# Turning the operands of a small DFT: the stationary side becomes x, column by column, and the table moves

## The chip, the cores and the metric

The kernel runs on one core of one Trainium2 chip. The metric is device time in microseconds (us), taken over several executions. The engines are named as in the profile: PE is TensorE (PEld its weight loads), DVE is VectorE, ACT is ScalarE, POOL is GpSimd, SP is SyncE. "Lxx" is a line of the kernel that was profiled. Line numbers differ from kernel to kernel, so the text says which line does what.

## The reference

```python
def _attn_ref(x):                       # x: 8 x 3136 x 256, float32
    X = np.fft.fft(x, axis=1)           # over the 3136 positions = 49 x 64
    X = np.fft.fft(X, axis=2)           # over the 256 features
    return X.real

def _moe_ref(x, U, V, w_ch1, w_ch2):    # U: 3136x32, V: 32x3136, w_ch1: 256x1024, w_ch2: 1024x256
    h = x.transpose(0, 2, 1) @ U @ V    # low-rank mixing over the positions
    u = x + h.transpose(0, 2, 1)
    return u + np.maximum(u @ w_ch1, 0) @ w_ch2
```

The transform over 3136 = 49 x 64 is done in two stages. The first is a DFT over the 49 rows n1 (position = 64 n1 + n2). It leaves, for each of the 64 values of n2 and each of 25 values of k1 (the rest follow by symmetry), one vector over the features d. The second stage is a DFT over n2. A matmul of this kernel sums over partitions (its stationary operand has 98 of them in the first stage, 2 x 49), so the first stage wants n1 on the partitions, and the second wants n2 there. What lies on the partitions for the second stage is called the *lines*: 32 cosine and 32 sine lines, because n2 and 64 - n2 are folded together.

## The kernel before

The batches are handled in four pairs. Pair 0 is special: its two batches go one after the other, so that PE has something to do early. For these the first stage is `s1_single`. The table is the stationary operand, x moves, and the result `z` has k1 and the cosine/sine index on the partitions and the lines along the free axis. To bring the lines onto the partitions, z is written to DRAM and read back (`turn`). The argument calls this round trip "the turn".

```python
    def load_single(b, c):                       # a quarter of one batch: 49 rows, and 49 mirrored rows
        ...
        nc.gpsimd.dma_start(out=xs[0:PR:2], in_=x_pn[r, 8 * c:8 * c + 8, :])
        mirror = bass.AP(x.tensor, x.offset + (b * S + N2 - 8 * c) * D, [[N2 * D, N1], [-D, 8], [1, D]])
        nc.gpsimd.dma_start(out=xs[1:PR:2], in_=mirror)
    ...
    def s1_single(pr, b, tiles, evacs, engines):
        def step(n, s):
            ...                                  # two column tiles of 64, in turn; 98x64 table stationary
                        nc.tensor.matmul(o, f, y, start=(m == 0), stop=True, skip_group_check=True)
            evacs[n](z[:, 2 * s:2 * s + 2, :], ps[:])
            if n % 2:
                ...                              # z to DRAM, two lines at a time
                    engines(n)[i].dma_start(out=dst, in_=z[64 * i:64 * i + 64, 4 * q:4 * q + 4]...)
        for n, s in enumerate([2, 3, 4, 5, 6, 7, 1, 0]):
            yield lambda n=n, s=s: step(n, s)

    def turn(pr, b, parts, engines=(nc.sync,)):
        g = gpool.tile([P, NK1, D], BF16, tag=f"g{b}", name="g")
        src = zd[pr.p % 2, b].rearrange("k cn d -> cn k d")
        for i, (k0, k1) in enumerate(parts):     # back from DRAM, lines on the partitions
            engines[i % len(engines)].dma_start(out=g[0:64, k0:k1], in_=src[:, k0:k1, :])

    def te_single(pr, b, spread):                # the product with U from g: tile "teps"
        ...                                      # then te is copied below g by "spread"
    def s3_steps(pr, b, evac):                   # second stage: g stationary, table T moving
        ...
```

After that come the two MLP products (`hps`, `ops`), in chunks. Each pair has 52 slots, and `plan` hangs other work on the slots. For pair 0 it places the work of the second batch (batch 1) thus:

```python
            place(s1_single(cur, 1, part[1], [copy_act, copy_dve] * 4, ...), 2, 10)
            place([lambda: turn(cur, 1, whole)], 10, 11)
            place([lambda: te_single(cur, 1, spread_pool)], 15, 16)
            place(s3_steps(cur, 1, copy_dve), 17, 29)
            place_next(pairs[1], 8, 2.6, 44)
```

The first batch (batch 0) is done before the slots begin, in what I call the front.

## Time and profile before

| | before |
|---|---|
| time, median of 3 executions (range) | 476.18 us (475.4 to 478.35) |
| span of the profiled execution | 472.8 us |
| PE busy | 440.1 us (93%) |
| first second-stage product (L290) | starts at 32.4 us |
| product with U of batch 1 (teps) ends | 81.7 us |

The first part of the page gives the busy time of each engine, its share of the span, and its instructions:

```profile
PE 440.1 (93%) x3831; PEld 310.1 (66%) x3831; DVE 224.4 (47%) x520; ACT 287.6 (61%) x387; POOL 139.0 (29%) x140
```

PE is nearly full on average. The places where it is not are the only ones that an early change can win. The chain of waits shows two of them. Its columns are the start, the duration, and what the time went to (lines that follow each other in the chain, cut to 0 to 85 us):

```profile
20.09 3.52 DMA zturn<-z
...
24.31 5.91 DMA g<-zturn
30.26 0.69 PE teps L266 x18
...
32.41 0.54 PE ps L290 x4
...
67.12 2.41 DMA zturn<-z
69.58 9.20 DMA g<-zturn
78.82 2.87 PE teps L266 x48
81.68 1.82 PE hps L341 x4
```

Twice the chain leaves PE and follows the turn: at 20 to 30 us for batch 0, and at 67 to 79 us for batch 1. The same shows in the waits of PE (line and what it waited for: us in total, times, longest), for 0 to 110 us:

```profile
PE teps L266 <- DMA g<-zturn: 6.8, 2, 6.5
```

The stop at 72 to 79 us costs more than its 6.5 us, because PE's granted clock is about half in the stretch behind it. A window shows it. Its columns are the stretch and its length, the busy time of PE, PEld, DVE, ACT and POOL (with instructions), then PE's granted clock (1.00 is full speed), the DMA share and GB/s:

```profile
79.00:84.00 5.00, 5.00 (x60) 3.61 (x57) 2.23 (x5) 0.46 (x1) 3.70 (x3) 0.53 0.71 201
```

At half clock the teps products take 2.87 us, and four hps matmuls take 1.82 us, not 0.97.

### The profile page before, as it was taken

What the parts mean: (1) busy time and instruction counts of PE and PEld (TensorE: products, weight loads), DVE (VectorE), ACT (ScalarE), POOL (GpSimd) and SP (SyncE); (2) the same over time, 40 slices, a digit from 0 to 9 for tenths busy, and PEclk for the clock granted to TensorE, in tenths of its full rate; (3) what the DMA queues carried; (4) which work ended last, traced back from release to release, by engine and by line L of the source; (5) the groups of instructions that cost most, each with busy time, mean ns of one, the idle gap of its engine ahead of it and who ended that gap; (6) DMA issues with size and microseconds to landing.
All of it is one profiled execution on the core that took longest, in us unless ns stands there. A gap on an engine that the chain in (4) does not pass through costs nothing.

```text
span 472.8 us, 9751 instructions
## 1 busy us (share of the span) xinstructions
PE 440.1 (93%) x3831; PEld 310.1 (66%) x3831; DVE 224.4 (47%) x520; ACT 287.6 (61%) x387; POOL 139.0 (29%) x140
## 2 busy tenths in 40 slices
PE   6679994899999999999999999999999999999993
PEld 2445663677767776677777767677767777767672
DVE  8965431767326366646244366654245345112111
ACT  6436561577755657677665656777565655666660
POOL 8442522945150054643060145452130000000000
PEclk9978997999999999999999999999999999999998
DMA  9969369678478366585493366584682222233323
GB/s 158 229 159 161 87 179 192 171 235 215 143 175 196 91 169 155 138 258 180 124 219 89 102 171 182 140 259 150 150 153 63 68 64 66 68 76 75 79 57 79
DMA packets 69298, 67.65 MB, mean 143 GB/s; under 512 B 17396, under 2 KB 62268, under 8 KB 69220
## 3 DMA queue, kind: packets, MB, share of 16 engines
q1 hardware_dynamic: 55252, 47.43, 40.9%
q0 software_dynamic: 11168, 12.92, 12.4%
q10 hardware_dynamic: 2832, 6.69, 3.9%
q8 instruction: 30, 0.49, 0.5%
q14 instruction: 16, 0.13, 0.1%
HBM read 35.95 MB, written 34.28 MB: 149 GB/s over the span
## 4 chain that ended last, share of the span: by engine, by line
PE 79%; DVE 8%; DMA 6%; ACT 3%; issue 2%; SPq 0%; DVEq 0%; ACTq 0%
PE hps L341 33%; PE ops L352 32%; DMA g<-zturn 5%; PE ops L355 4%; PE ps L290 4%; PE ps L172 2%; ACT hT L343 2%; DVE q L79 2%; PE teps L252 1%; DMA zturn<-z 1%; PE ps L216 1%; PE teps L266 1%; DVE ob L362 1%; ACT om L361 1%; DVE yb L122 1%
## 5 line engine op out<-in xcount | busy, mean ns | idle before, releaser
L343 ACT ACTIVATE hT<-hps 128x1024 bf16<-128x1024 f32 (+1 forms) x208 | 202.5, 975 | 138.3 <-PE hps L341 136.9
L352 PE MATMUL ops<-W,hT 128*128 128x256 bf16 x1568 | 224.6, 273 | 0.0
L352 PEld LDWEIGHTS <-hT 128*128 128x128 bf16 x1568 | 145.3, 98 | 34.4 <-issue 0.3
L362 DVE TENSOR_TENSOR ob<-ops,om 128x256 f32<-128x256 f32 (+1 forms) x100 | 41.8, 418 | 196.0 <-ACT om L361 194.2
L341 PE MATMUL hps<-q,W1p 128*128 128x512 bf16 (+1 forms) x448 | 106.7, 361 | 1.0 <-DVE q L79 0.7
L341 PE MATMUL hps<-q,W1m 128*128 128x512 bf16 x384 | 98.9, 381 | 0.5 <-ACT hT L343 0.5
L131 POOL TENSOR_TENSOR y<-xa,xb 98x1020 f32<-98x1020 f32 (+1 forms) x24 | 55.2, 2299 | 127.8 <-DMA xa<-in_x_dram 115.4
L79 DVE CAST q<-ps 128x512 bf16<-128x512 f32 (+3 forms) x120 | 64.4, 558 | 29.6 <-PE ps L290 26.6
L341 PEld LDWEIGHTS <-W1p 128*128 128x128 bf16 x448 | 40.4, 98 | 29.2 <-issue 4.7
L341 PEld LDWEIGHTS <-W1m 128*128 128x128 bf16 x384 | 35.8, 98 | 26.8 <-issue 2.2
L355 PEld LDWEIGHTS <-q 128*128 128x128 bf16 x392 | 38.5, 98 | 21.0 <-issue 0.3
L76 ACT CAST z<-ps 128x512 bf16<-128x512 f32 x57 | 33.4, 586 | 14.3 <-PE ps L172 12.5
L361 ACT COPY om<-ops 128x256 f32<-128x256 f32 (+1 forms) x100 | 36.8, 368 | 8.0 <-PE ops L352 7.6
L363 DVE TENSOR_TENSOR ob<-ops,om 128x256 f32<-128x256 f32 (+1 forms) x100 | 40.9, 409 | 0.0
L290 PE MATMUL ps<-T,g 128*128 128x128 bf16 (+1 forms) x400 | 38.2, 223 | 2.8 <-DVE g L274 1.5
L355 PE MATMUL ops<-Bp,q 128*128 128x128 f16 x200 | 38.4, 219 | 0.0
L355 PE MATMUL ops<-Bm,q 128*128 128x128 f16 x192 | 37.0, 219 | 0.0
L274 POOL COPY g<-te 64x1024 int32<-64x1024 int32 (+1 forms) x21 | 22.0, 1092 | 46.5 <-DVE te L238 46.5
L290 PEld LDWEIGHTS <-g 128*128 128x128 bf16 x400 | 30.3, 100 | 8.1 <-issue 2.0
L122 DVE TENSOR_TENSOR yb<-y 98x508 bf16<-98x508 f32 (+1 forms) x24 | 26.9, 1123 | 0.0
L102 POOL DMA_INDIRECT xb<-in_x_dram,idx x24 | 25.0, 1041 | 5.4 <-issue 3.9
L172 PE MATMUL ps<-yb,F 98*128 98x258 bf16 (+1 forms) x108 | 18.9, 265 | 4.9 <-DVE q L79 4.9
(126 smaller groups left out, 205.1 us busy)
## 6 DMA issues: line engine op xcount, KB each, us to landing
out_dram<-ob SPq DMA_DIRECT2D x392, 64.0 KB
xa<-in_x_dram SPq DMA_DIRECT2D x24, 392.0 KB
g<-zturn SPq DMA_DIRECT2D x7, 800.0 KB
zturn<-z ACTq DMA_DIRECT2D x9, 512.0 KB
xs<-in_x_dram POOLq DMA_DIRECT2D x16, 196.0 KB, 8.3
w_f<-in_moe_w_ch_dram SPq DMA_DIRECT2D x2, 1024.0 KB
zturn<-z SPq DMA_DIRECT2D x15, 128.0 KB
zturn<-z ACTq DMA_DIRECT2D x3, 448.0 KB
```

The source lines that it names most:

```text
L76: nc.scalar.copy(o, i)
L79: nc.vector.tensor_copy(o, i)
L122: nc.vector.tensor_tensor(o[:, :, 1:128], i[:, :, 1:128], i[:, :, 255:128:-1], op=AL.add)
L131: nc.gpsimd.tensor_tensor(ck.y[:, 0:n, 1:256], ck.xa[:, 0:n, 1:256], rb[:, :, 255:0:-1], op=AL.add)
L290: nc.tensor.matmul(o, lt, r, start=st, stop=True, skip_group_check=True)
L341: nc.tensor.matmul(ps[:, i, 0:n], (W1p if ch.sg > 0 else W1m)[:, blk, j], q[:, blk, c0:c0 + n], start=(blk == 0), stop=(blk == 1))
L343: nc.scalar.activation(ch.h[:, 2 * jp:2 * jp + 2, 0:n], ps[:, :, 0:n], AF.Relu)
L352: nc.tensor.matmul(ps, ch.h[:, j, t * P:(t + 1) * P], W2[:, j, :], start=(j == 0 and t % 2 == 0), stop=(j == JT - 1), skip_group_check=True)
L355: nc.tensor.matmul(ps[:, j], q[:, j, tk], (Bp if ch.sg > 0 else Bm)[:, j], start=False, stop=False, skip_group_check=True)
L361: nc.scalar.copy(om[:, 0:n], ch.po[:, 0:n, 1])
L362: nc.vector.tensor_tensor(ob[:, 0:n, 0:P], ch.po[:, 0:n, 0], om[:, 0:n], op=AL.add)
L363: nc.vector.tensor_tensor(ob[:, 0:n, P:D], ch.po[:, 0:n, 0], om[:, 0:n], op=AL.subtract)
```

## The change

The intent is to have the first stage's result come out of PE with the lines already on the partitions. For this x is the stationary operand: for each feature d, the 98 x 32 block X[0:98, :, d] is loaded as weights, and the table moves (50 columns, real and imaginary parts of 25 k1). The result's partitions are then the lines. Four 32-column tiles of the array are used in turn. A batch takes 512 pairs of a weight load and a matmul, in place of 8 steps with wide matmuls. The turn is gone for pair 0. What it needs in exchange: the whole of x of a batch in one tile before the first pair, line 32 on its own path, the lines in reversed order, and a row of signs in the table T. The diff, cut to its core:

```diff
-    def load_single(b, c):
...
+    def load_single(b):
+        X = zpool.tile([P, 32, D], BF16, tag="z", name="X")
+        nc.vector.memset(X[0:PR, 31, :].bitcast(FP32), 0.0)
...
+        rows(0, L, 33, 1, X[1:2 * L:2, 0:31, :])              # L = 48 rows
+        rows(0, L, 31, -1, X[0:2 * L:2, 0:16, :])             # 48 rows, lines backwards
+        rows(0, L, 15, -1, X[0:2 * L:2, 16:32, :])
+        rows(L, 1, 33, 1, X[PR - 1:PR, 0:31, :])              # the 49th row
+        rows(L - 1, 2, 31, -1, X[PR - 4:PR:2, 0:32, :])       # rows 48 and 49, backwards
+        nc.gpsimd.dma_start(out=x32[b][0:PR:2], in_=x_pn[r0:r0 + N1, 32, :])
...
-    def s1_single(pr, b, tiles, evacs, engines):
...
+    def turned_products(X, ps, i0, n):
+        for i in range(n):
...
+            for m in range(2):
+                for h in range(2):
+                    d = 64 * h + i0 + i
+                    for c in range(2):
+                        o = ps[64 * h + 32 * c:64 * h + 32 * c + 32, i]
+                        w = X[0:PR, :, (256 - d if d else 128) if m else d]
...
+                        nc.tensor.matmul(oc, w, f, start=first[2 * h + c], stop=True, skip_group_check=True)
...
+    def turned_out(g, ps, i0, n, evacs):
+        for h in range(2):
+            evacs[h](g[0:63]..., ps[64 * h:64 * h + 63]...)    # straight into g
...
+    trow = tmp([1, NK1, 64], "trow", BF16)                     # row of signs for T, by POOL
...
+    nc.sync.dma_start(out=T[63:64, :, 0:64], in_=trow[:])
...
+    sin_of(T[0:63, :, 0:64], ta2[0:63], 18)
...
     nc.vector.tensor_copy(T[0:64, :, 64:128], T[0:64, :, 63::-1])
+    for r in range(4):                                         # the front: batch 0, 128 pairs a round
+        ps = psh.tile([P, 16, 2, 32], FP32, tag="h", name="tps")
+        turned_products(X0, ps, 16 * r, 16)
+        turned_out(g0, ps, 16 * r, 16, [copy_dve, copy_act])
...
-    for c in (1, 2, 3, 0):
-        part[1][c] = load_single(1, c)
+    loads = load_single(1)                                     # at the end of the front
...
-            place(s1_single(cur, 1, part[1], ...), 2, 10)
-            place([lambda: turn(cur, 1, whole)], 10, 11)
+            place(turned_steps(cur, 1, X1, [copy_act, copy_dve]), 4, 12)   # batch 1, 64 pairs a step
```

The loads of w_ch1, w_ch2 and V also moved to POOL's queue, behind x.

## The prediction

> **What bounds the kernel now.** The page gives PE 93% of a 472.8 us span; from about 84 us on PE is hardly idle, and the change does not touch that part. What can be won lies in two waits for the first pair's turn through DRAM. (1) Front: the chain of waits shows zturn<-z 3.5 us, an issue of 0.6, then g<-zturn 5.9, until 30.2 us; the first mixing product that reads g (L290) starts at 32.4. (2) Batch 1: in the timeline PE stops at about 72 us and resumes with teps at 78.8, released by g<-zturn (6.6 us idle). The granted clock is then half: 50 teps matmuls take 2.87 us, the next four hps 1.89 instead of 1.03. I count 8.8 us in all. A like half clock covers 32.5 to 39.3 us (eight hps take 3.68 us).
>
> **Removed.** Both turns, eight evacuations a batch (0.59 to 0.69 us) and, for batch 1, eight first-stage steps of 0.56 us = 4.5 us of PE.
>
> **Added.** Per batch 512 small load-and-multiply pairs (98x32 stationary, 50 moving columns, four column tiles in turn), and evacuations of 400 or 800 elements: by the casts in the trace (512 elements 0.69 us on DVE, 0.59 on ACT) an estimated 0.6 and 1.1 us each, beside PE. The price of a pair decides. In the trace two column tiles start 2 to 4 ns apart and each streams at its own pace (254 columns every 108 ns); L252 sustains a pair per 27.9 ns, bounded by the array. [...] the uups matmuls here (64 columns, one tile) start 31.6 ns apart. [...] stationary columns 512 bytes apart and instruction fetch (256 instructions per 1.0 to 1.7 us packet here) should push it up. Estimate: 10 to 18 ns, centre 14, 7 us a batch.
>
> **On the critical path.** Front: products can start at about 17 us, when x has landed and the U products are through, and end near 24.5; then DVE still has the last evacuation, W1p (1.2 us), the residual tables (1.9), the T copies and teps before L290. I expect L290 at 31 to 32, hardly earlier. Batch 1: 8.8 + 4.5 - 7.2 = 6 us won. Against it: the turned products need all of X1, while before chunks were used as they landed. X1's loads (10 us of packets in front now) follow a DVE memset behind the te spreads, so X1 may land only at 45 to 49 us and PE may wait a few us at step 4. Net about 5 us.
>
> **Predicted: 471 us**, 8 in 10 between 461 and 481; faster by over 2% 0.32, within 2% 0.58, slower by over 2% 0.10.
>
> **What would show it.** zturn traffic of pair 0 gone; no PE gap before the second teps, full granted clock from 70 to 84 us; turned matmuls under 20 ns apart; L290 starting at 30 to 33 us with DVE as its releaser; a PE wait at the first batch-1 turned product, released by the X load; after 90 us the same lines as before.
>
> **What would make it wrong.** Pairs at 28 ns or more (14 us a batch: nothing left, or a loss); X1 so late that PE stalls over 5 us and loses the clock again; or pairs at 7 ns and a front 3 us shorter, which gives 462.

The marks stand where two passages on the price of a pair are cut: a figure that no run here shows, and a floor for a pair that was partly taken from it. The uups matmuls' 31.6 ns in one tile make 7.9 ns over four tiles, if four run side by side as two do at L252 (128 columns, at 254 columns in 108 ns, take 54 ns, so 27 ns a pair with two tiles; 27.9 were measured). What was added to that for the strides and the instructions, up to the centre of 14 ns, was the author's estimate. The sum itself came to 8.8 + 4.5 - 7.2 = 6 us won at batch 1 (7.2 us is 512 x 14 ns), about 5 us after a late X1: 476 - 5 = 471 us.

## The result, and the profile after

| | before (4 runs) | after (4 runs) |
|---|---|---|
| time, median (range) | 476.0 us (475.4 to 478.35) | 494.6 us (492.66 to 495.14) |
| ratio, with 95% interval | | 1.0371 (1.0327 to 1.0414), slower |
| span of the profiled execution | 472.8 us | 493.4 us |
| first second-stage product | 32.4 us (L290) | 45.0 us (L307) |
| product with U of batch 1 ends | 81.7 us | 102.5 us |

A ratio is the mean time of one kernel's runs over that of the other's runs of the same rounds, so not quite the ratio of the medians quoted. Executions over 1.5% slower than the fastest of the same kernel are left out of the means.

The last two rows of the table already locate the loss. It is 12.6 us at the first second-stage product and 20.8 us when the product with U of batch 1 ends. The spans differ by 20.6 us, so nothing is lost or won later. The page's first part shows 884 more matmuls on PE, each with its weight load:

```profile
PE 449.7 (91%) x4715; PEld 322.0 (65%) x4715; DVE 225.9 (46%) x524; ACT 290.4 (59%) x394; POOL 135.6 (27%) x134
```

The chain of waits after (the turn's lines are gone; other things stand in their place):

```profile
23.04 5.79 DMA T<-trow
28.92 0.58 DVE T L576
29.50 0.90 DVE g L80
...
31.30 4.82 PE tps L222 x223
36.15 0.99 DVE g L80
...
44.29 0.70 DVE g L291
45.04 0.57 PE ps L307 x4
...
50.98 0.53 POOL X L118
51.51 7.91 DMA X<-in_x_dram
59.42 2.57 issue
...
62.66 3.45 DMA x<-in_x_dram
...
101.01 1.52 PE teps L283 x47
```

And the waits of PE after:

```profile
PE ps L198 <- DMA x<-in_x_dram: 7.9, 1, 7.9
PE tps L222 <- ACT g L77: 5.8, 1, 5.8
PE ps L307 <- DVE g L291: 4.3, 1, 4.3
...
PE tps L222 <- issue: 2.4, 1, 2.4
```

Both early waits that the change was to remove are gone, and new ones have come. In the front, the rounds of pairs (tile tps, L222) run from 18.3 to 36.1 us, with a stop for the evacuations of two tiles (the copies from the accumulators into g). DVE copies one half of each tile and ACT, after it, the other; and in its order DVE stands before them at a copy of T (L576), which waits for the row of signs (28.83 us; the copy starts at 28.92, the first evacuation behind it at 29.50). From the last round to L307 pass another 9 us, about 7 on DVE and 2 on ACT. At batch 1, PE comes to the first product (L198, that of line 32) at 58.3 us and waits 7.9 us for the x of batch 1, called X1 here; its last load, the small one of line 32 (`x<-in_x_dram`), lands at 66.1 us. The window from 60 to 70 us shows the half clock again, now here:

```profile
60.00:70.00 10.00, 3.85 (x78) 2.61 (x78) 0.58 (x1) 1.23 (x3) 1.77 (x4) 0.52 0.21 25
```

In that window the DMA engines are nearly idle (25 GB/s), so X1 is late because it was asked for late. The timeline of POOL, which issues the loads, says why (start, us, engine, line, operation, count, and the idle time before with its releaser):

```profile
1.42 2.77 POOL L118 DMA_DIRECT2D X<-in_x_dram  x4
14.05 0.69 POOL L118 DMA_DIRECT2D X<-in_x_dram  x1 [9.86 <-DMA X<-in_x_dram]
...
50.98 2.53 POOL L118 DMA_DIRECT2D X<-in_x_dram  x4 [24.29 <-issue]
61.99 0.68 POOL L118 DMA_DIRECT2D X<-in_x_dram  x1 [8.49 <-issue]
```

Each batch has five loads into X, and line 32's behind them. The fifth, the small one with two rows, writes elements of partition 94 that the mirrored loads of 48 rows also write. I take this to be why POOL holds it, and everything that POOL has behind it, until those have landed (e5 below speaks for it: 2.97 us of waiting in place of 9.86). For batch 0 this delays all of POOL's later work by 9.9 us, the row of signs included; for batch 1 it comes on top of a late start, which a DVE memset at 50.3 us sets. There the view names no releaser for the 8.49 us, and the chain has the load before landed at 59.42 us, 2.57 us before POOL goes on; that rest is not explained.

### The profile page after: what moved, and what is told of

Read it like the earlier page. It is cut to its first block, busy times and chain, and to the rows that moved or that the text cites. A ratio compares the mean times of both kernels' runs of the same rounds, so it can differ in the third digit from the quotient of the medians.

```text
span 493.4 us, 11483 instructions
## 1 busy us (share of the span) xinstructions
PE 449.7 (91%) x4715; PEld 322.0 (65%) x4715; DVE 225.9 (46%) x524; ACT 290.4 (59%) x394; POOL 135.6 (27%) x134
## 2 busy tenths in 40 slices
DMA packets 59506, 64.02 MB, mean 130 GB/s; under 512 B 13764, under 2 KB 52510, under 8 KB 59326
## 3 DMA queue, kind: packets, MB, share of 16 engines
q1 hardware_dynamic: 49086, 41.61, 36.8%
q0 software_dynamic: 8208, 15.38, 13.4%
## 4 chain that ended last, share of the span: by engine, by line
PE 75%; DMA 6%; DVE 5%; ACT 3%; issue 3%; SPq 1%; POOL 0%; DVEq 0%; ACTq 0%
PE ops L369 30%; PE hps L358 30%; PE ops L372 4%; PE ps L307 4%; PE ps L222 2%; PE ps L179 2%; ACT hT L360 2%; DMA X<-in_x_dram 2%; DMA g<-zturn 1%; DMA out_dram<-ob 1%; PE teps L269 1%; DVE q L80 1%; DMA T<-trow 1%; PE tps L222 1%; SPq L384 1%
## 5 line engine op out<-in xcount | busy, mean ns | idle before, releaser
L372 PEld LDWEIGHTS <-q 128*128 128x128 bf16 x392 | 38.4, 98 | 22.1 <-issue 1.6
L307 PE MATMUL ps<-T,g 128*128 128x128 bf16 (+1 forms) x400 | 38.3, 223 | 6.6 <-DVE g L291 4.3
L372 PE MATMUL ops<-Bp,q 128*128 128x128 f16 x200 | 38.4, 219 | 0.0
L307 PEld LDWEIGHTS <-g 128*128 128x128 bf16 x400 | 30.4, 101 | 12.0 <-DVE g L291 4.5
L77 ACT CAST z<-ps 128x512 bf16<-128x512 f32 x48 | 28.2, 588 | 12.3 <-PE ps L179 12.1
L222 PEld LDWEIGHTS <-X 98*32 98x32 bf16 x1024 | 19.8, 172 | 10.3 <-issue 9.9
```

The lines of the kernel that those rows point to most:

```text
L77: nc.scalar.copy(o, i)
L222: nc.tensor.matmul(oc, w, f, start=first[2 * h + c], stop=True, skip_group_check=True)
L307: nc.tensor.matmul(o, lt, r, start=st, stop=True, skip_group_check=True)
L372: nc.tensor.matmul(ps[:, j], q[:, j, tk], (Bp if ch.sg > 0 else Bm)[:, j], start=False, stop=False, skip_group_check=True)
```

## The experiments

The causes that the result offered were put as theories. W: waits for late data (the row of signs behind POOL's wait, and X1) are the loss. D: the tail of DVE work between the last round and L307 is. F came up after the first experiments: PE isn't supplied with instructions fast enough. P: the pairs themselves cost more than the 14 ns predicted. The quoted expectations use these letters.

Twelve kernels ran, in four groups, each group on one chip with the kernel before beside it. The medians of before in the groups were 474.15, 473.23, 474.73 and 474.31 us. Ratios in this section are against those runs. The kernel "after" itself was not run again; where I subtract from its 494.6 us the numbers come from two chips, whose runs of before differ by 2 to 3 us.

| run | what | median us | ratio (95% interval) |
|---|---|---|---|
| e1_copy_late | after, T's copy behind the rounds | 494.44 | 1.0453 (1.0355 to 1.0550) |
| e2_no_overlap | after, mirrored loads of 47 rows | 613.18 | 1.2939 (1.2825 to 1.3053) |
| e3_load_early | after, X1 loaded right behind the rounds | 486.67 | 1.0274 (1.0163 to 1.0384) |
| e4_all_three | e1, e2 and e3 together | 600.04 | 1.2688 (1.2569 to 1.2807) |
| e5_tail_first | after, two-row load first | 488.88 | 1.0361 (1.0299 to 1.0424) |
| e6_three_mended | e1, e3 and e5 together | 481.60 | 1.0208 (1.0149 to 1.0268) |
| e7_twice | e6, batch 1's pairs done twice | 490.46 | 1.0386 (1.0307 to 1.0466) |
| e8_second_only | before, the change for batch 1 alone | 474.79 | 1.0075 (0.9998 to 1.0151) |
| e9_te_before_w1 | e6, front's tail reordered | 482.46 | 1.0163 (1.0111 to 1.0216) |
| e10_before_te_late | before, batch 1's U product four slots later | 485.07 | 1.0207 (1.0154 to 1.0259) |
| e11_contiguous | e6, stationary from neighbouring elements (wrong result) | 476.26 | 1.0029 (0.9980 to 1.0078) |
| e12_second_gathered | e8, DVE gathers the columns first | 487.60 | 1.0313 (1.0268 to 1.0358) |

### e1_copy_late: the copy that waits for the row of signs, moved away

```diff
-    nc.vector.tensor_copy(T[0:64, :, 64:128], T[0:64, :, 63::-1])
     g0 = gpool.tile([P, NK1, D], BF16, tag="g0", name="g")
...                                                            # the four rounds
+    nc.vector.tensor_copy(T[0:64, :, 64:128], T[0:64, :, 63::-1])
     nc.scalar.copy(T[64:96, 1:9, 64:128], Vk[64:96, 48:40:-1, :])
```

> One line moved: the mirrored copy T[0:64,64:128] on DVE goes behind the evacuations of the turned rounds, so that the late landing of the row of signs (T<-trow, 28.9 us) no longer holds the in-order DVE queue. Theory W (waits: the loss is three waits that the change brought in): the turned rounds no longer wait 5.8 us for an evacuation, L307 starts about 6 us earlier (39 instead of 45 us) and the time falls by 5 to 8 us, to 487-490. Theory P (price: the loss is the PE time of 1024 small pairs at 15 to 18 ns, 17 us, less the 9 us of steps they replaced): the rounds are as long as before in PE time, what is not waited for at the front is waited for later, and the time falls by less than 2 us.

It took 494.44 us: nothing won, although the wait for the evacuations (5.8 us) is gone. L307 starts at 45.3 us. The waits of PE name another thing in the same place, and the timeline of PE in e1 shows where it sits (start, us, engine, line, operation, tiles, shapes, count, and the idle time before with its releaser):

```profile
PE tps L222 <- issue: 6.7, 3, 3.1
```

```profile
24.58 2.53 PE L222 MATMUL tps<-Fs,X 98*32 98x50 f16 x128 [2.69 <-issue]
30.23 2.57 PE L222 MATMUL tps<-Fs,X 98*32 98x50 f16 x128 [3.12 <-issue]
33.68 2.40 PE L222 MATMUL tps<-Fs,X 98*32 98x50 f16 x121 [0.88 <-issue]
```

"issue" means that PE waited for nothing that the profile shows. The pauses come after every 128 pairs, which is 256 instructions. I worked out the next table from the trace: PE's start times, counted as instructions, and the packets of the queue that carries instructions (16,384 bytes each; the page of after lists 37 such packets, and 2 x 4715 / 256 = 36.8; for before it lists 30, and 2 x 3831 / 256 = 29.9; so a packet seems to hold 256 of PE's instructions).

```
e1: PE stops after instruction   from     to       for     packet on the instruction queue
             448                 21.67    24.58    2.91    21.79 to 23.04
             704                 26.86    30.23    3.37    27.83 to 28.95
             960                 32.55    33.68    1.13    31.33 to 32.39
```

The times are from the start of one instruction to the start of the next, so a little longer than the idle times above. Each stop has its packet: PE goes on 1.3 to 1.5 us after that packet has ended. This is theory F.

A round is 128 pairs too, so the stops might belong to the rounds. They do not: each comes 7 pairs into a round (512 - 121 - 128 - 128 = 135 = 128 + 7). The trace of after has both kinds of stop side by side, one at pair 135 without a releaser and one at pair 256, where a round ends, for the evacuation:

```profile
18.36 2.42 PE L222 MATMUL tps<-Fs,X 98*32 98x25 f16 x132
23.20 2.35 PE L222 MATMUL tps<-Fs,X 98*32 98x50 f16 x121 [2.42 <-issue]
31.30 4.79 PE L222 MATMUL tps<-Fs,X 98*32 98x50 f16 x256 [5.75 <-ACT g L77]
```

Behind the second the marks 704 and 960 pass without a stop: while PE stood still a packet had come (27.53 to 28.66 us), and the next (31.04 to 32.21) came in time. So the late row of signs had hidden the supply, since both hold PE at the same time. Of W, the part about the row of signs falls as a cause by itself.

### e2_no_overlap and e4_all_three: without the shared partition, by 47 rows

```diff
-        rows(0, L, 31, -1, X[0:2 * L:2, 0:16, :])
-        rows(0, L, 15, -1, X[0:2 * L:2, 16:32, :])
+        rows(0, L - 1, 31, -1, X[0:2 * L - 2:2, 0:16, :])
+        rows(0, L - 1, 15, -1, X[0:2 * L - 2:2, 16:32, :])
```

> The two big mirrored loads of X take 47 rows instead of 48, so that the two-row load behind them writes no partition that they write. Theory W: POOL no longer waits 9.9 us at its fifth load; kio, V, the weights and the row of signs are all issued about 8 us earlier, T<-trow lands before 22 us; L307 starts 5 to 8 us earlier. For batch 1 the load of x32 is issued at about 54 instead of 62.7 us and the first turned product starts some 3 us sooner after the loads begin. Time down by 7 to 11 us, to 484-488. Theory P: down by less than 2 us.

> All three edits. Theory W, with the pairs still at their price: L307 starts at 36 to 39 us (before the change 32.4), no wait for X1, teps of batch 1 end at 86 to 89 us (before 81.7), time 478 to 483, so that what remains over the 476 of before is the price of the pairs and the DVE chain between the last round and L307. If it comes out under 474, the waits were the whole loss and the pairs cost nothing net; if over 488, the waits were a minor part (theory P).

Both miss their aim: 613.18 and 600.04 us. PE waited 129.7 us for x in e2. The DMA issues of after and then of e2 (transfer, queue, operation, count, KB each, median us from issue to landing) show what happened:

```profile
X<-in_x_dram POOLq DMA_DIRECT2D x4, 384.0 KB, 9.3
```

```profile
X<-in_x_dram POOLq DMA_DIRECT2D x4, 376.0 KB, 37.2
```

One row less went with a load four times slower. Between 20 and 38 us of e2, with these loads under way, the DMA engines are 9% busy and move 12 GB/s. On the whole page of e2 the queue software_dynamic has 53,264 packets for 15.53 MB, where that of after has 8,208 for 15.38 MB; why one row makes this difference was not shown. These two runs do not settle what the shared elements do: in e2 POOL stands still for 33.1 us before its third load, although no two loads write the same elements there, and the view names no releaser.

### e3_load_early: X1's loads right behind the rounds

```diff
         turned_out(g0, ps, 16 * r, 16, [copy_dve, copy_act])
+    loads = load_single(1)
+    X1 = next(loads)
+    for _ in loads:
+        pass
...
     bp_sin()
-    loads = load_single(1)
-    X1 = next(loads)
-    for _ in loads:
-        pass
```

> The zeroing and the loads of X for batch 1 stand right behind the turned rounds of batch 0 (when the buffer is free) instead of behind the te spreads. Theory W: the loads begin at about 37 instead of 51 us and have landed by about 53 us, the 7.9 us wait of PE before the first batch-1 turned product (58.3 to 66.2 us) goes, and the cold clock after it; time down by 8 to 10 us, to 485-487. Theory P: less than 2 us.

It took 486.67 us, 7.9 less than the 494.6 of after and 7.8 less than e1, which ran on the same chip. L307 is where it was (45.6 us). The loads begin at 38.4 us, not at 51.0, and PE's wait for X1 shrinks from 7.9 us to 0.6. So the late X1 was worth about 8 us, as W has it for batch 1.

### e5_tail_first: POOL's hold is taken away by order

```diff
+        rows(L - 1, 2, 31, -1, X[PR - 4:PR:2, 0:32, :])
         rows(0, L, 33, 1, X[1:2 * L:2, 0:31, :])
+        rows(L, 1, 33, 1, X[PR - 1:PR, 0:31, :])
         rows(0, L, 31, -1, X[0:2 * L:2, 0:16, :])
         rows(0, L, 15, -1, X[0:2 * L:2, 16:32, :])
-        rows(L, 1, 33, 1, X[PR - 1:PR, 0:31, :])
-        rows(L - 1, 2, 31, -1, X[PR - 4:PR:2, 0:32, :])
```

> The two-row load of X goes first and the single-row one before the mirrored ones, so that POOL waits only for a small early load; sizes as in the change (48 rows). Theory W (POOL's 9.9 us wait at its fifth load delays the front): POOL is through its loads at 7 to 9 us, the row of signs lands before 22 us, no PE wait for an evacuation in the turned rounds, L307 at 38 to 40 us. Theory F (after the run with the copy moved: PE stops after its instructions 448, 704 and 960, 256 apart, each time with a 16 KB packet on its instruction queue; in the front the supply of instructions bounds the turned rounds, about 4.2 us per 128 pairs): the rounds still take 14 to 17 us from first to last product and stop at 256-instruction marks; L307 at 41 to 44 us. Both: x32 of batch 1 is loaded about 3 us sooner, so the wait there shrinks from 7.9 to 4-5 us. Time 485 under W, 487-491 under F.

It took 488.88 us, 5.7 less than after. POOL now waits 2.97 us for a small load, not 9.86 for large ones. The wait stands in front of the first mirrored load, which is again the second of two loads that write the same elements of partition 94. The rounds last from 19.6 to 33.1 us, so 13.5 us for 512 pairs, or 26 ns a pair, though nothing holds PE but the stops at 448, 704 and 960 instructions (1.2, 1.5 and 1.7 us). L307 starts at 43.0 us, 2.1 us earlier than after. The other 3.4 us or so are X1's: its wait fell from 7.9 to 4.5 us. L307 and the time lie where F put them, not W.

### e6_three_mended: e1, e3 and e5 together

The edit is that of e1, e3 and e5.

> Tail first, loads of batch 1 early, mirrored copy late. Theory W: 476-479, theory F: 479-484 (the 486.7 of the early load less what the front gains). No wait for X1; PE in the rounds is stopped at 256-instruction marks, not by evacuations.

It took 481.60 us: 13.0 us less than after, and 8.4 us more than before in its own group. All the late data is gone from the list of waits. The stops stay, and so does the wait of L307 for DVE. First the waits of PE in e6, then its timeline:

```profile
PE ps L307 <- DVE g L291: 4.9, 1, 4.9
PE tps L222 <- issue: 4.0, 3, 1.6
```

```profile
23.50 2.58 PE L222 MATMUL tps<-Fs,X 98*32 98x50 f16 x128 [1.60 <-issue]
26.95 2.52 PE L222 MATMUL tps<-Fs,X 98*32 98x50 f16 x128 [0.87 <-issue]
30.95 2.38 PE L222 MATMUL tps<-Fs,X 98*32 98x50 f16 x121 [1.49 <-issue]
```

The packets of instructions now start at 20.81, 24.60, 28.50 and 32.28 us, 3.8 us apart, with hardly another transfer beside them (0 GB/s in most slices of the DMA view). That is the pace of the rounds: 256 instructions in 3.8 us is 30 ns a pair. At 20.81 us PE has begun about 350 of its instructions, so the packet that it needs after 448 comes with no long lead.

### e7_twice: the price of a pair in its place

```diff
             turned_products(X, ps, 8 * r, 8)
+            turned_products(X, ps, 8 * r, 8)
             turned_out(g, ps, 8 * r, 8, evacs)
```

Only batch 1 is doubled. The second set restarts the sums, so the result is right.

> As e6_three_mended, but each of the eight batch-1 steps runs its 64 pairs twice (the second pass starts its banks anew, so the result is right): 512 pairs more in the PE-bound stage. If a pair costs what it shows inside a run of pairs (15.2 ns), the time rises by 7.8 us over e6_three_mended; if instruction supply (256 instructions in 3.5 us, the pace of the fetches seen with idle DMA) bounds, a pair costs up to 27 ns and the time rises by 11 to 14 us; if pairs are hidden under other waits, by less than 4 us.

It took 490.46 us, 8.9 more than e6 on the same chip: 8.9 us / 512 = 17.3 ns a pair. In the traces of after and e6 the starts are 18.3 ns apart over a whole step of 64 pairs (17.4 to 18.9); the 15.2 ns of the expectation is the fastest stretch of 40 pairs in after, in a round of the front. So the price in place is at the top of the range predicted (10 to 18), and 3 to 4 ns over its centre. In the slots, MLP products (128 to 512 columns a matmul) stand between the steps, and the supply of instructions nearly keeps up: e6's packets are about 5 us or more apart there, and no idle time put down to issue exceeds 0.3 us. It is not so in every run: e7, whose packets are 3.4 to 5.7 us apart there, has one such stop of 0.5 us inside a step, and after, e1, e3, e9 and e11 have 0.6 to 1.3 us in all.

### e8_second_only: before, with the change for batch 1 alone

The edit puts `load_turned`, `line32`, `turned_products`, `turned_out` and `turned_steps` into the kernel before (lines in rising order, two-row load first), and:

```diff
-        part[1][c] = load_single(1, c)
+    X1 = load_turned(1)
...
-            place(s1_single(cur, 1, part[1], [copy_act, copy_dve] * 4, lambda n: (nc.sync, nc.sync)), 2, 10)
-            place([lambda: turn(cur, 1, whole)], 10, 11)
+            place(turned_steps(cur, 1, X1, [copy_act, copy_dve]), 4, 12)
```

> The kernel before, with the change for batch 1 alone (X1 in ascending line order, loads right after the first teps as before, tail first; batch 0 and the front as before). Expected from both theories: the 6.6 us stop before the second teps and the cold clock after it go (8.8 us), 4.5 us of old steps go, 512 pairs at 18 ns (9.4 us) come: 470 to 474 against 474-476 of before. If it is over 478, the pairs cost more in place than the trace shows; if the X1 load is late again, a PE wait at the first turned product shows it.

It took 474.79 us against 473.23, a ratio of 1.0075: no gain that shows. The stop before the second teps is gone, and teps runs at full clock. In before and then in e8, the timeline of PE has:

```profile
78.82 2.87 PE L266 MATMUL teps<-g,us 64*32 64x129 bf16 x50 [6.55 <-DMA g<-zturn]
```

```profile
80.27 1.59 PE L341 MATMUL teps<-g,us 64*32 64x129 bf16 x50
```

Yet it ends at 81.9 us, where it ended at 81.7 before. What was removed is worth the 8.8 us that the prediction counted. A new step takes 1.47 us, where an old one took 0.56; for eight steps that is 7.3 us. PE also waits 1.0 us for a fold of W2 at about 45 us, where before has old steps. That sums to 8.3 us, 0.5 us less than is removed. From the first second-stage product to the end of that teps e8 takes 1.0 us less than before (48.3 and 49.3 us). This product itself comes 1.1 us later, but the work before it is unchanged, and in e10 and e12, which share it, it comes 1.8 and 0.2 us later, so I count that as scatter between executions.

### e9_te_before_w1: the DVE tail of the front cut up

The edit moves T's copies and the residual tables between the rounds' evacuations, and the product with U before the products of W1:

```diff
         turned_out(g0, ps, 16 * r, 16, [copy_dve, copy_act])
+        if r == 0:
+            nc.vector.tensor_copy(T[0:64, :, 64:128], T[0:64, :, 63::-1])
+        if r == 1:
+            bp_sin = residual_tables()
...
+    te_single(first, 0, spread_first)
     for c in range(2):                                # W1 products
...
-    te_single(first, 0, spread_first)
```

> e6_three_mended with the front's tail in another order: teps, its copies and the first spread directly after the turned rounds, the W1 products behind them on PE, the residual tables and the T copies between the evacuations of the rounds, where DVE waits 2 to 3 us each time. Theory D (after the rounds the in-order DVE queue, not PE, holds L307: 43.1 us although the rounds end at 33.3 and teps at 38): L307 starts at 37 to 38 us and the time falls by 4 to 6 us to 476-478. Rival (PE's instruction supply is the whole cost of the front): L307 comes no more than 2 us earlier and the time stays at 480-482.

It took 482.46 us: no gain over e6 that shows (the two ran on two chips; each against its own before, they are 7.7 and 8.4 us over). L307 does start 2 us earlier, at 40.8 us, but the product with U of batch 1 starts at 89.7 us, 1.3 us later than in e6. The granted clock was at half for most of 23 to 40 us here, and batch 0's teps took 2.87 us, not 1.59. Yet this isn't where the lead goes: PE is still 1.8 us ahead of e6 at 65 us. It loses 2.7 us between 65 and 71 us, at one step of batch 1, where PE stops three times without a releaser (0.28, 0.39 and 0.44 us, beside and behind a packet of instructions, 64.02 to 65.35) and then has half the clock from 67.5 to 71.0 us. So D isn't refuted: in this order an earlier L307 was worth about 2 us until a later stop took it. What ends up of it without that stop was not measured.

### e10_before_te_late: could before have had the gain by waiting less?

```diff
-            place([lambda: te_single(cur, 1, spread_pool)], 15, 16)
-            place(s3_steps(cur, 1, copy_dve), 17, 29)
+            place([lambda: te_single(cur, 1, spread_pool)], 19, 20)
+            place(s3_steps(cur, 1, copy_dve), 21, 33)
```

> The kernel before, no part of the change; only teps of batch 1 is placed at step 19 instead of 15 and its s3 steps at 21 to 33 instead of 17 to 29, so that PE has other chunks to do while g<-zturn lands at 78.8 us. If the 6.6 us stop and the cold clock after it are a matter of where the consumer stands, the stop goes at no cost: 466 to 470 us. If the work behind it depends on g at once (the chunks from step 24 on), the stop moves and the time stays at 473-476.

It took 485.07 us, 10 more than before. The wait for the turn is gone, but POOL, which spreads te, now has pair 1's folds in front of it, and these wait for their loads:

```profile
PE ps L290 <- POOL g L274: 5.7, 1, 5.7
...
PE ps L172 <- DVE yb L124: 3.5, 1, 3.5
```

So the stop of before can't be filled by moving the U product by these four slots.

### e11_contiguous: how much of a pair is the way its weights are read

```diff
-                        w = X[0:PR, :, (256 - d if d else 128) if m else d]
+                        w = X[0:PR].rearrange("p l d -> p (l d)")[:, 32 * ((256 - d if d else 128) if m else d):][:, 0:32]
```

The stationary block has the same shape, but its 32 columns are neighbours in memory, where those of e6 lie 512 bytes apart. The result is wrong (relative error 0.67).

> e6_three_mended with the stationary operand of each turned pair read from 32 neighbouring elements instead of 32 elements 512 bytes apart; the result is wrong on purpose. If the strided read of the stationary operand sets the 15.2 ns of a pair inside a run, the run falls to 7-10 ns, and the eight batch-1 steps shorten by 2.5 to 4 us in all (time 477-479). If the issue of two instructions per pair sets it, it stays at 15 ns and the time at 480-483.

It took 476.26 us, 5.3 less than e6's 481.60 (on two chips; each against its own before, e11 is 1.5 us over and e6 8.4), and within 1% of before. Over most steps of batch 1 pairs start 7.7 ns apart, where e6 has 18.3. So about 10 of the 18.3 ns are the price of reading the weights from elements 512 bytes apart. That this is not the array's own pace shows in e6's rounds too: at a granted clock of 0.50 (27 to 31 us) its pairs start 17.9 ns apart, as in the slots at 1.00. In the first 28 pairs of a step of e11 four starts take 25 ns, later about 34; whether the matmul or the weight load of a pair sets the 25 ns is not shown. Of the 5.3 us, 2.3 are there before L307 (40.6 us, not 42.9) and 3.0 between it and the product with U of batch 1.

The front is a test of F. The pairs take half the time, yet the four rounds together take 11.6 us, where e6's take 14.2:

```profile
20.09 1.35 PE L222 MATMUL tps<-Fs,X 98*32 98x50 f16 x129
22.79 1.21 PE L222 MATMUL tps<-Fs,X 98*32 98x50 f16 x128 [1.35 <-issue]
26.52 1.42 PE L222 MATMUL tps<-Fs,X 98*32 98x50 f16 x128 [2.52 <-issue]
29.98 1.50 PE L222 MATMUL tps<-Fs,X 98*32 98x50 f16 x121 [2.04 <-issue]
```

The last round begins at 29.98 us, where e6 had 30.95. The packets start at 20.06, 23.89, 27.64 and 31.11 us, 3.5 to 3.8 us apart, as in e6, and the stops are at the same instructions (448, 704, 960). What PE no longer spends on pairs between the stops it spends on waiting; only the ends of the rounds get shorter. F stands. (No run changed the supply itself, with fewer instructions for the same work, for instance.) In both kernels, where one packet waits on the other, the 3.8 us are made up of the same three parts: the packet lasts 1.0 to 1.3 us, PE goes on 1.3 to 1.7 us after its end, and the next packet starts 1.1 to 1.6 us after that.

### e12_second_gathered: the columns gathered by DVE

e8 with two DVE copies a step, which put the columns of that step side by side in a small tile; PE then reads them as neighbours.

```diff
+                    nc.vector.tensor_copy(dst, by_d[:, 0:2, :, 8 * r:8 * r + 8])
...
-                        w = X[0:PR, :, (256 - d if d else 128) if m else d]
+                        w = Xc[:, m, h, i]
```

> e8_second_only (the change for batch 1 alone, 474.8 us) with one thing more: before each step DVE gathers the step's columns of X into a small tile in which the 32 lines of a column are neighbours (two copies of 512 elements, an estimated 1.2 us a step, one step ahead), so that each stationary operand is read from 32 neighbouring elements; the result is right. If the strided read is what a pair costs beyond the array's pace (15.2 against 6.2 ns in a run, as the contiguous run on wrong data showed, 5.3 us in all), and DVE has the room (about half idle from 44 to 75 us), the runs of pairs go to 7-8 ns and the time falls to 468-472, below the kernel before. If DVE's 10 us of copies delay its evacuations instead, it stays at 473-477.

It took 487.60 us, with a right result. Pairs do run at 7.7 to 11 ns over a step, but a copy of 512 elements took 1.3 to 2.1 us, and the two of a step mostly 2.6 us from the start of the first to the end of the second (they overlap), where I had estimated 1.2. Two lines of DVE's timeline, and PE's waits:

```profile
55.55 1.32 DVE L298 COPY xc<-X 98x512 bf16<-98x512 bf16 x1
56.47 1.67 DVE L300 COPY xc<-X 98x512 bf16<-98x512 bf16 x1
```

```profile
PE ps L276 <- DVE g L79: 3.8, 2, 1.9
...
PE ps L276 <- DVE xc L298: 2.3, 1, 2.3
PE ps L276 <- DVE xc L300: 2.2, 3, 1.0
```

DVE became what PE waits for. No version that ran beats the kernel before; e8 comes nearest with a right result.

## Why the prediction was wrong

The prediction said 471 us, with 461 to 481 as its range; 494.6 us was measured. Point by point:

1. *The price of a pair* ("10 to 18 ns, centre 14") held as a range, at its top: 17.3 ns in its place by e7, 18.3 ns over a step in the traces. The two reasons named were right: the strides account for about 10 ns (e11), and the supply of instructions sets the pace in the front (point 5).
2. *The stop before the second teps* and its half clock are gone, as predicted; after about 103 us the two kernels take the same time, also as predicted.
3. *"Batch 1: 8.8 + 4.5 - 7.2 = 6 us won"* is the first step that failed, in the size of one term. Done alone (e8), it won nothing that shows. The term for the added work was too small: eight steps took 8 x 1.47 = 11.8 us, not 7.2, because a step of 64 pairs takes 1.2 us at 18.4 ns and has about 0.3 us more around it. A wait of 1.0 us for the fold of W2 came to light as well: 8.8 + 4.5 - 11.8 - 1.0 leaves 0.5 us.
4. *"X1 may land only at 45 to 49 us and PE may wait a few us at step 4"* failed by size. X1's last load landed at 66.1 us, and PE waited 7.9 us. The mechanism, a DVE memset in front, was named rightly, but it came at 50.3 us, and I missed that POOL holds the fifth load until the first ones have landed (as I take it, because they write the same elements). e3 shows that it was worth about 8 us. Of the things that "would make it wrong" the prediction named this one.
5. *"Front: products can start at about 17 us [...] and end near 24.5"* is the largest failure. They ended at 36.1 us. The sum took the pair's own price, 14 ns. The front has no other work between the pairs, and there PE gets 256 instructions in about 3.8 us, so 30 ns a pair. The prediction named instruction fetch with "256 instructions per 1.0 to 1.7 us packet", but took the packet's duration for the pace; the packets start 3.5 to 3.9 us apart in the rounds of e6 and e11 (3.3 to 6.0 in e1, e5 and e7). The prediction's own case for a loss, "pairs at 28 ns or more", came true in the front, by the supply and not by the price of a pair. With the late row of signs and the weights' loads it was 17.8 us for 512 pairs; without them (e5) 13.5 us. Since e1 took only the wait for the row of signs away and won nothing, the weights' loads are left to account for the difference; that they delay the packets is argued (one interval of 6.0 us in e1), not shown.
6. *"I expect L290 at 31 to 32"* failed as a consequence. The tail of DVE work behind the last round was named, and DVE was the releaser, as predicted; it took 8.9 us (36.1 to 45.0) where the sum allowed about 7 (24.5 to 31 or 32).

Sum: +12.6 us at the first second-stage product and +8.2 us from there to the end of the second teps, against the spans' difference of 20.6 us. Mended (e6), it is +10.5 us in the front (42.9 against 32.4) and -2.1 us after it. With weights read from neighbouring elements (e11) it is about even. So the idea's gain in batch 1 exists but is small, and in the front the rounds, limited by instructions, and their tail are slower than the turn that they replace.

Left open: what sets the three parts of the 3.8 us from packet to packet; how much of the tail behind the rounds (9.6 us in e6) can be saved, since e9 lost its 2 us again; whether the columns can be brought together without loading DVE (by the load itself, for instance); and the clock in e9.

## What to carry to other kernels

Count instructions as well as array time: here 512 small pairs in a row with nothing long between them ran at the pace at which instructions arrived (256 in about 3.8 us, 30 ns a pair), and the same pairs spread among the MLP products ran nearly at their own price (17.3 ns). When a change removes a wait, ask what the removed work had covered and when its replacement's data is asked for: here the whole x of a batch was needed, and its last small load was issued only when the large ones had landed (at 61.99 us; the chain has the load before landed at 59.42). Before trusting a mending of one wait, look whether another wait lies under it at the same time (e1).
